# Moving ten of sixteen weight-conversion multiplies from ScalarE to GpSimd in an attention plus rational-FFN kernel

## The chip, the cores and the metric

The kernel runs on one core of a Trainium2 chip. The metric is the device time of one execution in microseconds. The core has a matrix engine (TensorE; PE in the profile, PEld its weight loads) and three engines that work on vectors: VectorE (DVE), ScalarE (ACT) and GpSimd (POOL). SyncE (SP) issues the transfers here. All engines run their own instruction queues and wait for each other by semaphores.

## The reference

Eight batches of eight heads: a packed attention of 32 queries `p` over 576 keys, then an attention of the 576 queries `q` over those 32 packed rows. The result, 4608 rows of 512, goes through a feed-forward layer with a rational activation. The two weight matrices come as float64.

```
p_packed = sm_attn(p, k, v)                 # 8 x 8 heads, 32 x 64 each
x        = sm_attn(q, p_packed, p_packed)   # 4608 x 512 after the transpose
h = x @ w_in                                # w_in  512 x 2048, float64
g = (a0 + a1 h + a2 h^2 + a3 h^3) / (1 + |b0||h| + |b1| h^2 + 1e-6)
out = g @ w_out                             # w_out 2048 x 512, float64
```

## The kernel before, in words

The feed-forward layer is walked in 128 units (batch, half of its rows, one of eight chunks of 256 hidden columns). `hidden` makes one unit: TensorE fills a PSUM tile `h`, of which there are two, ScalarE takes |h|, h² and a3·h+a2 from it, GpSimd adds `U` and `sq` (the denominator), ScalarE takes the logarithm and the exponential, and VectorE does the polynomial and the final products into `gh`, `gl` and `G`. The last VectorE products read the `h` tile and so release it for a later unit. `acc_block` multiplies a finished unit with its piece of `w_out` three units later (`LAG = 3`). The attention of a batch is split in steps that are spread between units; `m_chunk` multiplies its packed rows with `w_in`.

The weights arrive as 64-bit words. Sixteen pairs of 128-row or 256-column pieces (eight of `w_in`, eight of `w_out`; the list `words`) are loaded into borrowed buffers (`load_words`) and turned into float32 by `convert`, one pair each call: 128 partitions x 1024 words. A float64 word has a high and a low half of 32 bits, which lie side by side, so that each half is read at a step of two. The high half, read as float32, is multiplied in place by `REBIAS` = 2^-112, which moves its exponent to where float32 wants it; ScalarE scales the low half to an integer into the destination; VectorE takes the sign bits, shifts the high half left by three; and VectorE or GpSimd (GpSimd for odd pairs from the sixth on) adds the two. The first four pairs are converted after the instructions of the first attention (`PRE = 4`), one more at each unit, and more if one is due. By `words.sort` the pairs come in this order, counted from 0: `w_in` 0 to 3, `w_out` 0, 1, 2, `w_in` 4, `w_out` 3, `w_in` 5, 6, 7, `w_out` 4 to 7. Their buffers are `m` and `w`, so the profile calls the rebias of the high half `m<-m` or `w<-w` of type f32, the scaling of the low half `win<-m`, `win<-w`, `w<-w` or `half<-w` of type int32 from uint32, and the shift `m<-m` or `w<-w` of type int32.

The order of the instructions on each engine isn't the order of the program. `Planner` collects all operations, gives each a cost (`COST`, `cost`), models the time in which VectorE and GpSimd exclude each other (`shares`), simulates several list schedules (`schedule`, `order`) and emits the operations in the order of the best one. A GpSimd operation with fewer than three tensors is costed there at 135 ns plus 0.9 ns for each column. Where its plan leaves TensorE without work early in the kernel, `issue` puts in small multiplications by zero (line 290 in the profile); all planned operations are recorded at line 294.

Of the kernel before, what the change touches and what calls it, by code (L numbers as in the profile page):

```python
# [13 lines left out]
F32 = mybir.dt.float32  # L14
# [5 lines left out]
AF = mybir.ActivationFunctionType  # L20
ALU = mybir.AluOpType
# [6 lines left out]
REBIAS = 2.0**-112  # L28
# [4 lines left out]
class Planner:  # L33
# [8 lines left out]
    TRANSPOSE, F32 = (15, 0.734), (30, 1.62)  # L42
# [283 lines left out]
def attention_rational_ffn(  # L326
# [42 lines left out]
    nc = Planner(tc.nc)  # L369
# [77 lines left out]
    words_in, converted = [], 0  # L447

    def load_words(n):
        while len(words_in) < min(len(words), converted + n):  # L450
            r = len(words_in)
            kind, i, n2 = words[r]
            used = [x for x, _ in words_in]
            free = [x for x, end in room if r < end and x not in used[converted:]]
            free = [x for x in free if x[0] is not w_ring or x[1] not in (2, 3) or started]
            if not free:
                return
            x = min(free, key=lambda x: max((j for j in range(r) if used[j] == x), default=-1))
            raw = x[0].at(x[1], [P, n2 * 512], I64)
            if kind == "in":  # L460
                c = i // 2
                for y in range(2):
                    src = w_in[2 * y * P : (2 * y + 2) * P, c * CF : (c + 1) * CF].rearrange("(x p) f -> p x f", p=P)
                    nc.sync.dma_start(raw[:, 512 * y : 512 * (y + 1)].rearrange("p (x y) -> p x y", x=2), src)
            else:
                for y in range(n2):
                    nc.sync.dma_start(raw[:, 512 * y : 512 * (y + 1)], w_out[(i + y) * P : (i + y + 1) * P, :])
            words_in.append((x, raw))
# [3 lines left out]
    def undivided(c):  # L472
        if c not in X:
            pair = [i for i in UNDIVIDED if c in UNDIVIDED[i]]
            if pair:
                t = w_ring.at(pair[0], dtype=F32)
                X.update({y: t[:, x] for x, y in enumerate(UNDIVIDED[pair[0]])})
            else:
                X[c] = half_ring.at(c - 2)
        return X[c]  # L480
# [19 lines left out]
    def convert():  # L500
        nonlocal converted
        if converted == len(words):
            return
        load_words(AHEAD)
        (kind, i, n), raw = words[converted], words_in[converted][1]
        x = 4 if kind == "in" else n
        w = raw.bitcast(I32).rearrange("p (x y two) -> p x y two", x=x, two=2)
        lo, hi = w[:, :, :, 0], w[:, :, :, 1]

        if kind == "in":  # L510
            dst = win[:, i // 2]
            di = dst.bitcast(I32)
        else:
            dst = undivided(i // 2)
            di = dst.bitcast(I32)
        nc.scalar.activation(hi.bitcast(F32), hi.bitcast(F32), AF.Copy, scale=REBIAS)

        nc.scalar.activation(di, lo.bitcast(U32), AF.Copy, scale=2.0**-29)
        top = raw.bitcast(U16).rearrange("p (x y four) -> p x y four", x=x, four=4)[:, :, :, 3]
        sign = dst.bitcast(U16).rearrange("p x (y two) -> p x y two", two=2)[:, :, :, 1]  # L520
        nc.vector.tensor_scalar(sign, top, 0x8000, None, ALU.bitwise_and)
        nc.vector.tensor_scalar(hi, hi, 3, None, ALU.logical_shift_left)
        (nc.gpsimd if converted > 3 and converted % 2 else nc.vector).tensor_add(dst.bitcast(I32), hi, di)
        converted += 1
        load_words(AHEAD)
# [490 lines left out]
    for _ in range(PRE):  # L1016
        convert()
# [30 lines left out]
    for u in range(NU + LAG + 2):  # L1048
        if u < NU:
            pipe[u] = hidden(*units[u])  # L1050
        stage(u - 2)
        stage(u)
        if 0 <= u - LAG < NU:
            acc_block(u - LAG, 0)
        filler(2 * u)
        stage(u)
        stage(u - 1)
        for x in rem.get(u, ()):
            remainder(*x)
        convert()  # L1060
        while converted < len(words) and due(words[converted]) <= u + 1:
            convert()
        if 0 <= u - LAG < NU:
            acc_block(u - LAG, 1)
        if u in DIVIDE:
            divide(DIVIDE[u])
        filler(2 * u + 1)
# [78 lines left out]
```

## Time and profile before

| | |
|---|---|
| median of 3 runs | 765.33 us (764.8 to 766.16) |
| the profiled execution's own time | 765.33 us |
| its span, first to last instruction | 763.5 us |
| outside the span | 1.83 us |
| TensorE's granted clock, mean | 1.000 of full speed |

The profile is of one execution. Its busy times by engine say how full each queue was on the average; the stretches and the timelines say which was full when. On ScalarE and VectorE a recorded duration overlaps the next instruction's start, so that the step from one start to the next is the price that a full queue pays.

### The profile page before, as it was taken

How to read it: one execution, taken by the hardware profiler on the slowest of the kernel's cores; microseconds unless marked ns; L12 is line 12 of the kernel's file. 1: busy time of each engine (PE TensorE's matmuls, PEld its weight loads, DVE VectorE, ACT ScalarE, POOL GpSimd, SP SyncE). 2: the span in 40 equal slices, each digit the busy share in tenths (PEclk: the TensorE clock that was granted, in tenths of full speed). 3: DMA queues.
4: the chain of work that ended last, by engine and by line, in shares of the span. 5: the costliest groups of instructions: out<-in, count | busy, mean ns of one | idle time of the engine just before them, and what ended most of it. 6: DMA issues, size and time to landing. Idle time of an engine off the chain costs nothing.

```text
span 763.5 us, 15004 instructions
## 1 busy us (share of the span) xinstructions
PE 752.7 (99%) x5608; PEld 583.8 (76%) x5608; DVE 656.1 (86%) x1050; ACT 618.0 (81%) x1074; POOL 468.2 (61%) x457
## 2 busy tenths in 40 slices
PE   8899999999999999999999999999999999999997
PEld 7675645678788888778788887778788887778886
DVE  2889999998988889998998889998998888988773
ACT  5689986898787888988786888888786887897882
POOL 0035546986785556846695566855685655966662
PEclk9999999999999999999999999999999999999999
DMA  8994740204801137025701118122801015000001
GB/s 248 301 372 130 201 97 1 82 28 58 110 1 56 43 39 121 9 84 60 107 1 56 42 26 122 22 84 33 125 4 56 27 27 81 1 28 1 29 1 41
DMA packets 156632, 56.41 MB, mean 74 GB/s; under 512 B 126864, under 2 KB 145808, under 8 KB 156560
## 3 DMA queue, kind: packets, MB, share of 16 engines
q1 hardware_dynamic: 156560, 55.46, 33.3%
q8 instruction: 44, 0.72, 0.4%
q14 instruction: 28, 0.23, 0.1%
HBM read 46.01 MB, written 9.44 MB: 73 GB/s over the span
## 4 chain that ended last, share of the span: by engine, by line
PE 89%; DMA 4%; ACT 2%; DVE 2%; SPq 1%; POOL 1%; issue 1%; DVEq 0%; POOLq 0%; ACTq 0%
PE acc L294 46%; PE h L294 27%; PE at L294 15%; SPq L294 1%; DMA nat<-in_k_dram 1%; PE acc L290 1%; DMA w<-in_q_dram 1%; DVE Y L294 1%; DMA AH<-in_k_dram 1%; DMA w<-in_moe_w_out_dram 1%; ACT sq L294 0%; ACT U L294 0%; POOL U L294 0%; POOL gl L294 0%; ACT Y L294 0%
## 5 line engine op out<-in xcount | busy, mean ns | idle before, releaser
L294 POOL TENSOR_TENSOR U<-U,sq 128x576 f32<-128x576 f32 x128 | 185.5, 1449 | 139.2 <-ACT sq L294 135.9
L294 DVE SCALAR_TENSOR_TENSOR Y<-Y,abS,h 128x576 f32<-128x576 f32 x256 | 205.7, 804 | 55.0 <-ACT h L294 52.7
L294 PE MATMUL acc<-w,gh 128*128 128x512 f32 x736 | 240.7, 407 | 0.5 <-ACT half L294 0.5
L294 PE MATMUL h<-AH,m 128*128 128x288 f32 x1024 | 193.7, 313 | 0.7 <-DVE G L294 0.4
L294 PEld LDWEIGHTS h<-AH,m 128*128 128x128 f32 x1024 | 158.1, 188 | 28.5 <-DVE Y L294 7.1
L294 POOL TENSOR_TENSOR gl<-Y,gh 128x512 fp32r<-128x512 f32 x116 | 150.3, 1297 | 31.3 <-POOL G L294 13.6
L294 PEld LDWEIGHTS acc<-w,gh 128*128 128x128 f32 x736 | 133.6, 188 | 45.9 <-issue 16.5
L294 PE MATMUL acc<-w,gl 128*128 128x512 f32 x384 | 150.6, 411 | 0.0
L294 ACT ACTIVATE sq<-U,one 128x576 f32<-128x576 f32 x128 | 101.2, 790 | 34.9 <-POOL U L294 34.7
L294 ACT ACTIVATE U<-h 128x576 f32<-128x576 f32 x128 | 83.6, 653 | 40.3 <-PE h L294 39.9
L294 DVE TENSOR_TENSOR Y<-Y,h 128x576 f32<-128x576 f32 x128 | 95.2, 744 | 15.6 <-ACT Y L294 15.3
L294 ACT ACTIVATE h<-sq 128x576 f32<-128x576 f32 x128 | 85.1, 665 | 21.6 <-DVE Y L294 20.0
L294 PE MATMUL h<-AL,m 128*128 128x288 f32 x448 | 97.0, 296 | 0.0
L294 ACT ACTIVATE Y<-h,abS 128x576 f32<-128x576 f32 x128 | 96.7, 755 | 0.0
L294 DVE SCALAR_TENSOR_TENSOR h<-U,h 128x576 f32<-128x576 f32 x128 | 95.9, 749 | 0.0
L294 PEld LDWEIGHTS acc<-w,gl 128*128 128x128 f32 x384 | 71.8, 188 | 22.9 <-issue 10.2
L294 DVE SCALAR_TENSOR_TENSOR Y<-h,Y 128x576 f32<-128x576 f32 x116 | 86.9, 749 | 1.9
L294 ACT CAST gh<-Y 128x512 fp32r<-128x512 f32 x116 | 73.0, 629 | 14.7 <-DVE Y L294 10.1
L294 ACT ACTIVATE sq<-h 128x576 f32<-128x576 f32 x128 | 83.8, 654 | 0.0
L294 PE MATMUL acc<-half,gh 128*128 128x512 f32 x240 | 78.2, 409 | 0.2 <-ACT gh L294 0.2
L294 PEld LDWEIGHTS h<-AL,m 128*128 128x128 f32 x448 | 71.9, 188 | 2.1 <-issue 1.4
L294 PEld LDWEIGHTS acc<-half,gh 128*128 128x128 f32 x240 | 43.9, 188 | 13.5 <-issue 5.1
(149 smaller groups left out, 940.5 us busy)
## 6 DMA issues: line engine op xcount, KB each, us to landing
w<-in_moe_w_out_dram SPq DMA_DIRECT2D x16, 512.0 KB, 5.1
out_dram<-half SPq DMA_DIRECT2D x15, 512.0 KB, 2.9
nat<-in_k_dram SPq DMA_DIRECT2D x48, 144.0 KB, 4.3
nat<-in_q_dram SPq DMA_DIRECT2D x48, 144.0 KB, 4.3
nat<-in_v_dram SPq DMA_DIRECT2D x24, 256.0 KB, 3.3
m<-in_moe_w_in_dram SPq DMA_DIRECT2D x10, 512.0 KB, 9.2
w<-in_moe_w_in_dram SPq DMA_DIRECT2D x6, 512.0 KB, 8.9
nat<-in_k_dram SPq DMA_DIRECT2D x4, 512.0 KB, 7.2
```

Source lines behind the costliest of these rows:

```text
L290: getattr(self.nc.tensor, name)(*args, **kwargs)
L294: getattr(getattr(self.nc, engine), name)(*args, **kwargs)
```

## The change

For pairs 0 to 3 and for pairs 4, 6, 8, 10, 12 and 14 the multiplication of the high half by 2^-112 is issued to GpSimd as a `tensor_scalar`, on the same data in place. For the other six (5, 7, 9, 11, 13, 15) it stays on ScalarE. Nothing else in the program's text differs; the planner draws up the whole order anew with the operations on their new engine.

```
-        nc.scalar.activation(hi.bitcast(F32), hi.bitcast(F32), AF.Copy, scale=REBIAS)
+        if converted < 4 or converted % 2 == 0:
+            nc.gpsimd.tensor_scalar(hi.bitcast(F32), hi.bitcast(F32), REBIAS, None, ALU.mult)
+        else:
+            nc.scalar.activation(hi.bitcast(F32), hi.bitcast(F32), AF.Copy, scale=REBIAS)
```

## Rows read from the trace of the kernel before

**Rows 1.** The page: the span, and each engine's busy time over it.
```profile
span 763.5 us, 15004 instructions
...
PE 752.7 (99%) x5608; PEld 583.8 (76%) x5608; DVE 656.1 (86%) x1050; ACT 618.0 (81%) x1074; POOL 468.2 (61%) x457
```

**Rows 2.** Stretches: length, then busy us and instructions of PE, PEld, DVE, ACT, POOL.
```profile
29.30:41.40 12.10, 12.10 (x155) 9.27 (x140) 12.10 (x33) 7.58 (x15) 0.83 (x1) 1.00 0.89 260
41.20:82.20 41.00, 40.75 (x356) 26.69 (x354) 38.02 (x69) 40.65 (x67) 18.16 (x10) 1.00 0.71 234
82.20:100.60 18.40, 18.40 (x109) 9.73 (x109) 16.75 (x24) 18.30 (x35) 10.93 (x6) 1.00 0.89 194
...
126.00:763.00 637.00, 632.09 (x4558) 505.62 (x4558) 552.29 (x858) 518.15 (x902) 422.71 (x423) 1.00 0.27 48
```

**Rows 3.** Stretches, line 290 alone (TensorE's multiplications by zero): PE, then PEld.
```profile
41.20:82.20 41.00, 11.22 (x114) 8.90 (x112) 1.00 0.71 234
82.20:126.00 43.80, 0.05 (x1) 0.00 (x0) 1.00 0.44 103
```

**Rows 4.** Groups by form, whole span: the rebias on ScalarE, of the eleven pairs in `w`.
```profile
L294 ACT ACTIVATE w<-w 128x1024 f32<-128x1024 f32 x11 | 13.2, 1232 | 3.6 <-DMA w<-in_moe_w_out_dram 3.6
```

**Rows 5.** Groups by form, stretch 41.2 to 82.2: the rebias on ScalarE.
```profile
L294 ACT ACTIVATE w<-w 128x1024 f32<-128x1024 f32 x7 | 8.2, 1231 | 3.6 <-DMA w<-in_moe_w_out_dram 3.6
...
L294 ACT ACTIVATE m<-m 128x1024 f32<-128x1024 f32 x1 | 1.3, 1309 | 0.0
```

**Rows 6.** Timeline of ScalarE: start, duration, operation, idle before it.
```profile
33.39 1.18 ACT L294 ACTIVATE w<-w 128x1024 f32<-128x1024 f32 x1
...
34.96 1.18 ACT L294 ACTIVATE w<-w 128x1024 int32<-128x1024 uint32 x1
36.02 0.69 ACT L294 ACTIVATE kx<-kx 128x576 f32<-128x576 f32 x1
...
63.14 1.31 ACT L294 ACTIVATE m<-m 128x1024 f32<-128x1024 f32 x1
64.18 1.31 ACT L294 ACTIVATE w<-w 128x1024 f32<-128x1024 f32 x1
...
72.92 1.18 ACT L294 ACTIVATE half<-w 128x1024 int32<-128x1024 uint32 x1
...
74.10 0.71 ACT L294 ACTIVATE h<-sq 128x576 f32<-128x576 f32 x1
```

**Rows 7.** Timeline of VectorE.
```profile
34.23 0.75 DVE L294 TENSOR_TENSOR kx<-kx,small 128x576 f32<-128x576 f32 x1
...
59.62 1.25 DVE L294 TENSOR_SCALAR w<-w 128x1024 int32<-128x1024 int32 x1
...
69.98 0.71 DVE L294 TENSOR_TENSOR small<-small 128x4 f32<-128x4 f32 x1
...
74.01 1.53 DVE L294 TENSOR_SCALAR m<-m 128x1024 int32<-128x1024 int32 x1
...
75.52 0.81 DVE L294 SCALAR_TENSOR_TENSOR Y<-Y,abS,h 128x576 f32<-128x576 f32 x1
```

**Rows 8.** Tile `m` to 130 us: the shift's shortest, median and longest, in ns.
```profile
L294 DVE TENSOR_SCALAR m<-m x5: 675/701/1534, 17.9 to 74.0; 128x1024 int32<-128x1024 int32 x5
```

**Rows 9.** Groups by form, whole span: GpSimd's one-input copy and 1024-column two-input add.
```profile
L294 POOL COPY G<-Y 128x64 f32<-128x64 f32 x116 | 27.6, 238 | 36.4 <-DVE Y L294 35.6 <-ACT sq L294 0.9
...
L294 POOL TENSOR_TENSOR w<-w,w 128x1024 int32<-128x1024 int32 x3 | 7.2, 2410 | 7.0 <-DVE w L294 7.0
```

**Rows 10.** Timeline of GpSimd.
```profile
8.31 0.29 POOL L294 COPY pn<-pn 128x128 f32<-128x128 f32 x1 [6.98 <-DMA pn<-in_p_dram]
...
72.55 2.42 POOL L294 TENSOR_TENSOR win<-w,win 128x1024 int32<-128x1024 int32 x1
```

**Rows 11.** Stretches of two batches each, between the same transfers out.
```profile
263.30:436.50 173.20, 173.20 (x1320) 138.94 (x1318) 156.06 (x248) 143.34 (x254) 113.11 (x114) 1.00 0.34 57
436.50:610.30 173.80, 173.77 (x1320) 138.74 (x1318) 155.52 (x248) 143.47 (x254) 113.14 (x114) 1.00 0.32 56
```

## The prediction

> **What bounds the kernel now.** I read four views, from coarse to fine: the page, then stretches of the span, then what TensorE was given to do there, then the timelines.
>
> On the page TensorE is busy for 752.7 of 763.5 us, ScalarE for 618.0 and GpSimd for 468.2 [rows 1]. Taken alone this says that ScalarE doesn't matter. It is an average over stages, and the conversions all lie in one early stage: eleven rebias instructions work on `w` and the other five on `m` [rows 4], and eight of the sixteen start between 41.2 and 82.2 us [rows 5].
>
> By stretches there are three stages [rows 2]. From 29.3 to 41.4 VectorE is busy for all of 12.1 us, and ScalarE for 7.58. From 41.2 to 82.2 ScalarE is busy for 40.65 of 41.0 us and VectorE for 38.02. From 126 us on TensorE is busy for 632.09 of 637.0 us.
>
> TensorE looks busy in the middle stage as well, 40.75 of 41.0 us. The reader must see what it is busy with: 11.22 us of that are multiplications by zero, which the program puts where its plan has nothing for TensorE [rows 3]. From 82.2 to 126 there are 0.05 us of them. So up to 82.2 us TensorE waits for ScalarE and VectorE, and behind that it catches up on work that it already has. A microsecond gained ahead of 82.2 is kept, since TensorE has nothing idle in which it could be lost again; one gained on ScalarE behind 82.2 is hidden by TensorE's own queue.
>
> **The change part by part.** The profiled execution took 765.33 us, 1.83 more than its span, and is equal to the median of the runs; the sum is made against 765.33.
>
> *What ScalarE loses.* Where its queue is full, one rebias costs the step to the next start: 64.18 - 63.14 = 1.04 us [rows 6]. Ten go, 10.4 us. I count them by stage, with the order of the pairs.
> - Pairs 0 to 3 stand in the opening, up to about 30 us, where ScalarE has room. I take 0 for them.
> - Pair 4 is the one at 33.39. Behind it an exponential of the first attention starts at 36.02, though the subtraction that feeds it ended at 34.23 + 0.75 = 34.98 [rows 6, 7]. ScalarE was late by up to 1.04 us there. But VectorE, which has the next step, is full over this whole stretch. I take 0, and keep 1.04 as the other bound.
> - Eight rebias instructions lie in 41.2 to 82.2 [rows 5]: pairs 5 to 12. Pairs 6, 8, 10 and 12 move. ScalarE is relieved by 4 x 1.04 = 4.2 us where it is full.
> - Pair 14 comes behind 82.2. TensorE's queue covers it: 0, and 1.04 if that cover were gone.
>
> *What VectorE allows.* With 4.2 us less on ScalarE the next to be late is VectorE. In the stage it has 41.0 - 38.02 = 2.98 us of idle time [rows 2], and its work there doesn't shrink. So the stage can shorten by 2.98 us at most, before what follows.
>
> *What GpSimd adds.* The trace has no multiplication by a constant on GpSimd. Below it is bounded by the one-input copy: 0.238 us for 64 columns and 0.29 for 128 [rows 9, 10], so 0.052 us for 64 more, and for 1024 columns 0.238 + 15 x 0.052 = 1.02 us. Above it is bounded by the two-input add of 1024 columns on the same strided words, 2.41 us [rows 9]. One input is what it has in common with the copy, so I take 1.02; the program's plan reckons with 0.135 + 1024 x 0.0009 = 1.06. GpSimd has 41.0 - 18.16 = 22.84 us free in the stage [rows 2], and 4 x 1.02 = 4.1 fit.
>
> [...]
>
> *What GpSimd does to VectorE.* The shift at 74.01 takes 1.53 us; the median of its kind is 0.701 [rows 7, 8]. Just in front of it GpSimd began an add at 72.55 that ended at 74.97 [rows 10]; the shift ends at 75.54, that is 0.57 later. It stood still until GpSimd was done, and lost 0.83 us. Two more in the stage are long in this way: a shift of 1.25 us, 0.55 too long, and an operation on four columns of 0.71 us [rows 7], where I put the excess at 0.55 as well. That is 1.9 us over ten GpSimd instructions [rows 2], 0.2 us each. Four more cost VectorE 0.8 us; the bounds are 0, and 0.83 each, 3.3 us.
>
> [...]
>
> *The new waits.* The shift, and behind it all later VectorE work of the queue, now waits for GpSimd in place of ScalarE. On GpSimd the `U` addition of a unit can stand behind a rebias, and ScalarE's logarithm waits for it. In return the rebias no longer stands ahead of the low half on the same engine, so a pair can be ready about 1.04 us earlier. I count these as even. No transfer is added or moved in the program; a buffer comes free when its pair is added up, as before.
>
> *The sum.* The stage shortens by the smaller of ScalarE's relief, 4.2 us, and VectorE's room, 2.98 - 0.8 = 2.2 us. The forecast is 765.33 - 2.2 = 763.1 us.
>
> **How much the new order blurs it.** Every cost that changes makes the planner draw up the whole order anew. Two stretches of two batches each, with the same 1320 TensorE instructions, take 173.2 and 173.8 us [rows 11]: the same work in two orders differs by 0.6. Over the 637 us from 126 on, 3.7 times as long, that is 2.2 us if all differences add and 1.2 if they are independent (0.6 times the root of 3.7). So I blur each case by 1.2 us. A measurement of this kernel can tell about 0.2% from no change, 1.5 us.
>
> **The rivals.**
>
> *Hidden anyway.* ScalarE is full because the planner fills gaps with conversions, not because the units are held up by them. For it: two rebias instructions stand back to back at 63.14 and 64.18 [rows 6], which reads like filling. Against it: at 72.92 a low-half scaling of 1.18 us stands directly ahead of the exponential at 74.10 on which VectorE's product at 75.52 waits [rows 6, 7], so conversions do hold up units. [...]
>
> *Full relief.* VectorE's idle time isn't the limit, because the new order also takes blocked time out of it and uses the start: 4 x 1.04 in the middle stage and 1.04 by the exponential at 36.02, 5.2 us, to 760.1. For it: 11.22 us of TensorE time are free to be won [rows 3]. Against it: VectorE's full opening.
>
> *Slower: GpSimd's price.* The instruction takes 2.41 us, like the two-input add, and the plan thinks 1.06. Each of the four in the middle stage then delivers 1.35 us late, with a `U` addition behind it on GpSimd and a shift on VectorE waiting; ScalarE's and VectorE's queues stand in their planned order meanwhile. That is 4 x 1.35 = 5.4 us against the gain of 2.2: 765.33 + 3.2 = 768.5. It decides from the duration at which 4 x (d - 1.06) = 2.2, d = 1.61 us. For it: every GpSimd row of 1024 columns is at 2.41. Against it: the one-input copies.
>
> *Slower: the order.* GpSimd's multiplication is as cheap as a copy, but the new order of the long stage from 126 on is 2.2 us worse, and nothing is won in front: 767.5 [rows 11].
>
> **How the numbers follow.** The forecast at 763.1 has a chance of 0.50, hidden anyway 0.20, full relief 0.12, slower by GpSimd's price 0.12, slower by the order 0.06. Blurred by 1.2 us to either side, the forecast alone spans 761.9 to 764.3; a fifth of that, 0.11 of its 0.50, lies above 763.8, where it counts as no change. So faster by over 0.2%: 0.39 + 0.12 = 0.51; within it: 0.11 + 0.20 = 0.31; slower: 0.12 + 0.06 = 0.18. The range that leaves out no more than 2 in 10 goes from 759.8, just past full relief, to 767.4, short of the case of GpSimd's price and about at that of the order.
>
> **What would show each step.** ScalarE should have six f32 rebias instructions left and GpSimd ten new ones, near 1.0 us each; a mean over 1.6 makes the slower rival. ScalarE's busy time between the first `h` and about 80 us should fall by some 4 us for the same units, and VectorE's idle time there close to zero: if VectorE keeps its 2.98 us, VectorE wasn't the limit. TensorE's multiplications by zero should fall from 11.22 us by about the gain. The unit at which they cease should begin some 2 us earlier, and the end should move by as much; a difference that appears only behind 126 us is the order's and not the change's. [...] I am wrong if GpSimd's price is over 1.6 us, if the units' rhythm before 82 us stays although ScalarE has gaps, or if the long stage comes out different by more than 2 us.

## The result, and the profile after

The changed kernel takes 769.62 us (median of six runs, 768.73 to 771.11) against 765.75 us before in the same comparison: a ratio of 1.0055, 95% interval 1.0042 to 1.0069. It is slower by 3.9 us where 2.2 us less was forecast, and outside the range of 759.8 to 767.4. The profiled execution is the longest of the six, 771.11 us, 1.5 above the median, so differences between the two profiles are larger than those of the medians.

The page of the changed kernel, against [rows 1]:

```profile
span 769.3 us, 14938 instructions
...
PE 750.2 (98%) x5568; PEld 581.1 (76%) x5568; DVE 663.0 (86%) x1050; ACT 609.9 (79%) x1064; POOL 496.4 (65%) x467
```

ScalarE lost ten instructions and 8.1 us. GpSimd gained ten and 28.2 us, almost 3 us each. VectorE has the same 1050 instructions and is busy for 6.9 us longer: the timelines below show it standing still inside instructions.

The same stretches of the changed kernel as in [rows 2]:

```profile
29.30:41.40 12.10, 11.27 (x156) 7.89 (x141) 11.47 (x29) 5.67 (x12) 6.25 (x3) 1.00 0.87 219
41.20:82.20 41.00, 37.59 (x257) 24.50 (x256) 39.18 (x60) 35.38 (x59) 28.51 (x14) 1.00 0.73 240
...
126.00:763.00 637.00, 634.03 (x4547) 505.42 (x4547) 558.65 (x872) 522.09 (x909) 424.20 (x424) 1.00 0.26 47
```

In the middle stage ScalarE was relieved as intended, from 40.65 to 35.38 us of 41.0. Nothing came of it: VectorE has 60 instructions there in place of 69 and was busy for longer. A relieved ScalarE beside a slower stage means that ScalarE's queue doesn't limit the changed kernel there; whether it did before is asked below, by leaving its work out.

GpSimd's groups by form up to 135 us:

```profile
L294 POOL TENSOR_SCALAR w<-w 128x1024 f32<-128x1024 f32 x6 | 18.6, 3105 | 1.7 <-DMA w<-in_moe_w_in_dram 0.9 <-DMA w<-in_moe_w_out_dram 0.8
L294 POOL TENSOR_SCALAR m<-m 128x1024 f32<-128x1024 f32 x4 | 11.9, 2978 | 13.1 <-DMA m<-in_moe_w_in_dram 13.1
```

The new instruction takes 3.0 to 3.1 us. The forecast took 1.02 and had 2.41 as its upper bound [rows 9].

VectorE's timeline in the changed kernel, and below it GpSimd's at the same places:

```profile
62.83 1.34 DVE L294 TENSOR_SCALAR w<-w 128x1024 int32<-128x1024 int32 x1
...
67.40 2.38 DVE L294 TENSOR_SCALAR half<-w 128x1024 uint16<-128x1024 uint16 x1
...
78.63 1.26 DVE L294 TENSOR_TENSOR small<-small 128x4 f32<-128x4 f32 x1
```

```profile
60.54 3.08 POOL L294 TENSOR_SCALAR w<-w 128x1024 f32<-128x1024 f32 x1 [0.92 <-DMA w<-in_moe_w_in_dram]
...
66.75 2.41 POOL L294 TENSOR_TENSOR win<-w,win 128x1024 int32<-128x1024 int32 x1
...
77.42 2.45 POOL L294 TENSOR_TENSOR half<-w,half 128x512 fp32r<-128x512 f32 x1 [0.63 <-DVE G L294]
```

Add start and duration on both sides: the shift ends at 64.17, GpSimd's rebias at 63.62; the sign instruction at 69.78, GpSimd's addition at 69.16; the four columns at 79.89, GpSimd's addition at 79.87. Each VectorE instruction waited out a GpSimd one that had begun before it. The first is held by a moved rebias itself, the other two by additions that the program had before too and that now stand at other places.

TensorE's multiplications by zero fell from 33.34 us (332 instructions) to 28.93 (292) in the whole kernel, while the kernel became slower. The prediction had named their fall as a sign of the gain. They are put in where the plan sees a hole, so they tell what the plan thinks, not what was won, and once put in they run.

### The profile page after: what moved, and what is told of

It reads as the page before. It is cut to its first block, busy times and chain, and to the rows that moved or that the text cites. A ratio compares the mean times of both kernels' runs of the same rounds, so it can differ in the third digit from the quotient of the medians.

```text
span 769.3 us, 14938 instructions
## 1 busy us (share of the span) xinstructions
PE 750.2 (98%) x5568; PEld 581.1 (76%) x5568; DVE 663.0 (86%) x1050; ACT 609.9 (79%) x1064; POOL 496.4 (65%) x467
## 4 chain that ended last, share of the span: by engine, by line
PE 83%; DVE 6%; ACT 3%; issue 2%; DMA 2%; SPq 2%; POOL 1%; ACTq 0%; DVEq 0%; POOLq 0%
PE acc L294 44%; PE h L294 25%; PE at L294 14%; DVE Y L294 2%; SPq L294 2%; DVE small L294 2%; DMA m<-in_moe_w_in_dram 1%; DMA AH<-in_k_dram 1%; ACT sq L294 1%; DVE half L294 1%; ACT Y L294 1%; ACT U L294 1%; ACT kx L294 1%; DVE h L294 1%; DVE win L294 0%
```

## The experiments

Each ratio is against the kernel before, run on the same chip beside it. In the diffs, "moved" marks operations that are planned as one thing and issued as another, by a few lines in `issue`:

```
             waiting.discard(i)
+            if i in self.moved:
+                x = calls[0][1][0]
+                self.nc.gpsimd.tensor_scalar(x, x, REBIAS, None, ALU.mult)   # or as said below
+                continue
```

and in `convert`, behind the rebias, which is recorded for ScalarE as before:

```
+        if converted < 4 or converted % 2 == 0:
+            nc.moved.add(len(nc.ops) - 1)
```

The order is then the one of the kernel before, instruction by instruction on each engine, and only the engine of the ten differs.

### What the multiplication costs by itself

A kernel of single instructions, two of each kind (loops cut, notes added):

```
nc.gpsimd.tensor_scalar(high(t[0]), high(t[0]), 0.5, None, ALU.mult)           # ta: step of two
for m in (256, 512, 1024):
    nc.gpsimd.tensor_scalar(t[1][:, 0:m], t[1][:, 0:m], 0.5, None, ALU.mult)   # tb: dense
nc.gpsimd.tensor_copy(t[2][:, 0:1024], t[2][:, 1024:2048])                     # tc: dense
nc.gpsimd.tensor_copy(high(t[3]), ones)                                        # td: step of two
nc.gpsimd.tensor_tensor(high(t[4]), high(t[4]), ones, ALU.mult)                # te: step of two
nc.gpsimd.tensor_scalar(high(t[7]), high(t[7]), REBIAS, None, ALU.mult)        # th
```

> Leaves out the whole computation: only single instructions on 128 partitions, one after the other, to get their prices. Theory A (the price is that of the operation, a multiplication by a constant on GpSimd): dense 1024 columns cost near 3.0 us as the strided ones do, and a strided copy costs near 1.0. Theory B (the price is that of the step of two): dense 1024 columns cost near 1.0 us, and the strided copy is near 3.0 as well. A strided two-input multiplication should be near the 2.41 us of the add.

Groups by form of this kernel:

```profile
L40 POOL TENSOR_SCALAR ta<-ta 128x1024 f32<-128x1024 f32 x2 | 5.7, 2856 | 6.9 <-DMA ta<-in_q_dram 6.9
L55 POOL TENSOR_SCALAR th<-th 128x1024 f32<-128x1024 f32 x2 | 5.7, 2856 | 0.1
L43 POOL TENSOR_SCALAR tb<-tb 128x1024 f32<-128x1024 f32 x2 | 5.5, 2771 | 0.2
L49 POOL TENSOR_TENSOR te<-te,ones 128x1024 f32<-128x1024 f32 x2 | 4.8, 2386 | 0.1
L47 POOL COPY td<-ones 128x1024 f32<-128x1024 f32 x2 | 3.0, 1498 | 0.1
L43 POOL TENSOR_SCALAR tb<-tb 128x512 f32<-128x512 f32 x2 | 3.0, 1491 | 0.2
...
L45 POOL COPY tc<-tc 128x1024 f32<-128x1024 f32 x2 | 2.1, 1040 | 0.1
L43 POOL TENSOR_SCALAR tb<-tb 128x256 f32<-128x256 f32 x2 | 1.7, 850 | 20.8 <-DMA tb<-in_q_dram 20.7
```

From 256 to 1024 dense columns the multiplication grows by 1921 ns, 2.5 ns for each column; the step of two adds 85 ns, and the factor adds nothing. So the price is in the main the operation's own. The dense copy of 1024 columns costs 1.04 us, close to the 1.02 that the prediction worked out from small copies [rows 9, 10]. Written at a step of two, as the rebias is, a copy costs 1.50 us, so even for a copy 1.02 was too little. And a multiplication by a constant isn't priced like a copy at all: at the step of two it costs 2.86 us, more than a multiplication of two tensors, 2.39 us.

### What the plan knows

If the loss came from a plan that thinks 1.06 us, a plan with the measured price should mend it. Three kernels, for all ten pairs, for pairs 0 to 3 alone, and for the other six alone:

```
-            fixed, per = 135, 0.9
+            fixed, per = (150, 2.78) if name == "tensor_scalar" else (135, 0.9)
...
-        if converted < 4 or converted % 2 == 0:
+        if converted < 4:                                 # first four
+        if converted >= 4 and converted % 2 == 0:         # later six
```

> The changed kernel, with the plan told that the new GpSimd instruction takes 3.0 us in place of 1.06. Theory A (the loss comes from a plan that is wrong by 1.9 us for each of ten instructions): the loss goes, 765.7 or below, down to 763.5. Theory B (the loss comes from the 30 us of GpSimd time themselves, which hold VectorE's shared operations and the opening): 768 to 770, much like the changed kernel.

> Only pairs 0 to 3 on GpSimd, with the plan told 3.0 us. In the trace of the changed kernel the first hidden unit is 3 us late. If the opening makes that loss by itself, 768 to 769 here and the first h near 40 us; if the loss is made by the six later pairs, 765 to 766.

> Only pairs 4, 6, 8, 10, 12 and 14 on GpSimd, with the plan told 3.0 us. If the later pairs gain what the prediction said, once the plan knows the price, 763 to 764.5. If GpSimd's hold on VectorE eats the relief of ScalarE, 765.5 to 768.

All ten: 781.59 us, 1.0215 [1.0201, 1.0229]. The first four: 768.81, 1.0047 [1.0033, 1.0061]. The later six: 777.12, 1.0160 [1.0147, 1.0174]. The theory fell: with the right price the planner makes a far worse kernel. In the kernel with the first four the first two transfers out start at 143.32 and 167.61 us, as before (143.35 and 168.04), and only the third is late, 207.90 against 203.99. That is long behind the conversions, and so the order's doing. Why the planner draws so badly with a true price was not settled; these three can't tell the engine's effect from the order's. The next runs hold one of them fixed.

### Order and engine taken apart

One kernel with the old order and the ten multiplications issued to GpSimd (the diff above), and one with the order of the changed kernel and the ten issued to ScalarE, where `issue` calls

```
+                self.nc.scalar.activation(x, x, AF.Copy, scale=REBIAS)
```

> All engines keep the order of the kernel before (drawn up with the ten rebias operations on ScalarE); only the ten instructions themselves are issued to GpSimd, at their place in that order. Theory B (GpSimd's 30 us hurt by themselves): 768 to 773. Theory C (the change costs mostly by the new order of everything else): 764 to 766.5.

> The other half of that pair: all engines keep the order of the changed kernel (drawn up as if GpSimd did the rebias in 1.06 us), but the ten instructions are issued to ScalarE as before. Theory B: 765 to 767, most of the loss is gone. Theory C: 768 to 770, the loss stays.

| | ten on ScalarE | ten on GpSimd |
|---|---|---|
| order of before | 765.25 | 768.42, 1.0047 [1.0034, 1.0060] |
| order of after | 767.30, 1.0032 [1.0020, 1.0044] | 769.62, 1.0055 [1.0042, 1.0069] (against 765.75) |

By the medians each alone loses: the engine 3.2 us, the order 2.1, which lies between the two ranges expected for it. Together 3.9, somewhat less than the sum. Starts of the same transfers out, in us, show where:

| transfer | before | GpSimd, old order | ScalarE, new order | after |
|---|---|---|---|---|
| first | 143.35 | 146.58 | 144.78 | 147.76 |
| second | 168.04 | 171.27 | 169.59 | 172.57 |
| third | 203.99 | 207.23 | 208.24 | 211.19 |
| last whole batch | 610.28 | 613.32 | 613.44 | 616.33 |

These are single executions; the two with the new order ran 1.2 and 1.5 us above their medians, so the order's share reads larger in the last row (3.2 us) than by the medians (2.1). Go along the rows. From the first column to the second it is 3.23, 3.23, 3.24 and 3.04; from the third to the fourth 2.98, 2.98, 2.95 and 2.89. The engine costs 3 us in either order, all of it ahead of the first transfer, and hardly any is lost or given back later. The order costs 1.4 us ahead of the first transfer, 2.7 more between the second and the third, and about 1.1 comes back by the last. Stretches between these transfers, of the kernel with the new order on ScalarE and then of the changed kernel:

```profile
0.00:144.78 144.78, 134.37 (x1112) 83.33 (x1112) 117.02 (x212) 114.47 (x195) 59.93 (x50) 1.00 0.61 178
...
169.59:208.24 38.65, 38.63 (x313) 31.47 (x320) 34.54 (x55) 31.63 (x57) 26.76 (x28) 1.00 0.57 83
```

```profile
0.00:147.76 147.76, 134.68 (x1112) 83.89 (x1112) 124.24 (x212) 105.11 (x185) 91.48 (x60) 1.00 0.60 174
...
172.57:211.19 38.62, 38.62 (x313) 31.48 (x320) 34.54 (x55) 31.59 (x57) 26.75 (x28) 1.00 0.52 83
```

Ahead of the first transfer both do the same 212 VectorE instructions; beside GpSimd's ten they take 7.2 us longer. In the stretch shown behind it the two agree to 0.1 us. The new order's stretch of 38.6 us has TensorE full, as has the old one's of 35.95 us; so that stretch is long by what TensorE is given there and not by a wait, as far as the profile tells.

Is 2.1 us for an order large? Two kernels on ScalarE with the plan's price of the rebias changed by 5 ns, which only draws the order anew:

```
+            fixed += 5 * (kwargs.get("scale") == REBIAS)     # the other: -5
```

> The kernel before, with the plan's price of the rebias on ScalarE raised by 5 ns and nothing else: the same instructions on the same engines, in another drawn-up order. It prices the drawing itself. The prediction took 1.2 us to either side for this. If the order's share in the loss is of that kind, the time moves by 1 to 5 us to some side; if orders hardly matter, 764.5 to 766.

> The kernel before, with the plan's price of the rebias on ScalarE lowered by 5 ns and nothing else: a second sample of how much the drawing of an order moves the time by itself. Raised by 5 ns it gave 0.9989 (0.9978 to 1.0001). I expect 763 to 767; beyond that, the 2.1 us of the changed kernel's order would be no more than scatter.

764.30 us, 0.9989 [0.9978, 1.0001], and 764.70, 0.9996 [0.9987, 1.0006]. Two redrawn orders stay within 1 us, the first a little below the range expected if orders hardly matter. So 2.1 us isn't the ordinary scatter of these two draws, though two draws are few.

### What relief is worth

If ScalarE's full queue is the limit, taking the ten instructions away must bring what the prediction summed up. First with the old order, so that nothing else moves. The correction of the exponent goes into VectorE's sign instruction, whose median is 0.75 us in both kernels:

```
+            if i in self.moved:
+                continue
...
+        if converted < 4 or converted % 2 == 0:
+            nc.vector.tensor_scalar(sign, top, 0x8000, 0x4000, ALU.bitwise_and, ALU.bitwise_or)
```

Then the same with the order drawn anew, for ten and for all sixteen.

> The order of the kernel before, with the ten rebias instructions left out; the bit they set is put in by VectorE's sign instruction, which has a second operation free (and 2^30 is then part of the sum of the halves; numbers below 2^-126 would come out wrong). It prices ScalarE's relief alone. If ScalarE's queue sets the middle stage, as the prediction said, 761 to 763.5; if the conversions only fill its gaps, 764.5 to 766.

> The same ten rebias instructions left out in the same way, with a new order drawn up for it. If the relief is worth something and the planner can use it, at or below the kernel with the frozen order, 759 to 763; if a new order costs by itself, above it, 765 to 769.

> All sixteen rebias instructions left out of ScalarE (as with ten: VectorE's sign instruction sets the bit), with a new order. ScalarE loses 16.6 us of work in the first 113 us. If its queue were the limit anywhere there, 758 to 762; if its conversions only fill gaps, 763.5 to 766, the order's scatter aside.

Ten left out, old order: 765.08, 0.9993 [0.9983, 1.0003]. Ten, new order: 764.33, 0.9992 [0.9983, 1.0001]. Sixteen: 765.58, 1.0001 [0.9991, 1.0011]. No gain clear of the noise, three times; by the intervals 1.3 us at the most, where 2.2 were forecast. (The second lies between the two ranges expected for it.) In the first of them, the middle stage and ScalarE's waits from 41.2 to 100.6 us:

```profile
41.20:82.20 41.00, 40.40 (x350) 26.47 (x350) 37.71 (x67) 38.15 (x65) 17.33 (x10) 1.00 0.69 226
```

```profile
ACT w L297 <- DMA w<-in_moe_w_out_dram: 4.0, 1, 4.0
ACT U L297 <- PE h L297: 1.1, 2, 0.6
ACT kx L297 <- DVE small L297: 1.0, 1, 1.0
ACT h L297 <- DVE Y L297: 0.8, 1, 0.8
ACT ppT L297 <- PE at L297: 0.5, 1, 0.5
```

Before, ScalarE waited for that transfer (3.6 us, a wait that ends as the stage begins) and 0.3 us for `h`, and for nothing else. Now it waits for TensorE, VectorE and again TensorE in turn: the relief turned into waits for the others, piece by piece. The `h` tiles start 0.3 us earlier than before at 64.32 and 78.55 (64.61 and 78.83), 0.4 at 117.76 (118.19), and no more.

Was VectorE the limit in its place? The sign instruction of the ten pairs is left out, old order:

```
+        if converted < 4 or converted % 2 == 0:
+            nc.moved.add(len(nc.ops) - 1)        # behind the sign instruction; issue skips it
```

> The kernel before in its own order, rebias on ScalarE, but with VectorE's sign instruction of the same ten pairs left out (weights lose their signs): VectorE has about 10 x 0.65 = 6.5 us less to do, ScalarE as much as ever. If VectorE is what the early stage really waits for, as the long VectorE instructions suggest, 760 to 763.5. If the turn of the two h tiles sets the rhythm and neither engine's queue does, 764 to 765.5.

765.43, 0.9994 [0.9985, 1.0003]. VectorE's waits from 41.2 to 100.6 us:

```profile
DVE Y L297 <- ACT Y L297: 5.4, 5, 1.8
DVE Y L297 <- ACT h L297: 1.9, 3, 1.4
```

They were 2.6 and 1.1 before. The two engines hand each other work by turns, and either one's relief becomes a wait for the other.

What the two wait for in the end, the trace of the kernel before shows. First TensorE's waits from 41.2 to 126 us, then pieces of the chain of work that ended last (start, duration, what):

```profile
PE h L294 <- DVE G L294: 0.4, 1, 0.4
PE at L294 <- ACT m L294: 0.3, 1, 0.3
```

```profile
47.76 0.66 PE at L294 x4
...
75.76 2.43 PE acc L290 x28
...
78.45 0.45 PE acc L290 x4
78.90 2.14 PE h L294 x8
...
120.38 0.02 issue
```

From 47.76 to 120.38 us the chain lies on TensorE alone, and the multiplications by zero (line 290) are part of it. They were put into TensorE's queue when the order was drawn up and run in their turn, whether or not there is a hole by then: 332 before, 332 with the ten rebias instructions left out. With them TensorE waits for other engines for 0.7 us in all in 84.8 us. In the middle stage, TensorE's multiplications by zero with ten rebias instructions left out, and the whole stage with ten sign instructions left out:

```profile
41.20:82.20 41.00, 10.79 (x108) 8.63 (x108) 1.00 0.69 226
```

```profile
41.20:82.20 41.00, 41.00 (x360) 27.15 (x359) 36.28 (x66) 40.26 (x66) 17.72 (x10) 1.00 0.71 229
```

By this reading TensorE's queue, filled up by multiplications by zero, sets the pace of the old order there, and a shorter queue on ScalarE or VectorE has nothing to win. It is read from the traces and not tested: a kernel without these multiplications was not run, and what the relief would be worth then stays open.

Then I relieved both: no rebias and no sign for any pair, order drawn anew.

```
-        nc.scalar.activation(hi.bitcast(F32), hi.bitcast(F32), AF.Copy, scale=REBIAS)
-        nc.vector.tensor_scalar(sign, top, 0x8000, None, ALU.bitwise_and)
```

> Both instructions are left out for all sixteen pairs, the rebias on ScalarE and the sign on VectorE (and the shift goes right in place of left, which keeps the numbers finite; the weights are wrong), with a new order. ScalarE has 16.6 us less to do in the early stage and VectorE about 10.4. If the two queues limit the stage together, each filling the other's gaps, 755 to 761. If the turn of the two h tiles or TensorE's own work limits it, 762.5 to 765.5.

764.27, 0.9981 [0.9971, 0.9990]: 1.0 us between the medians and 1.4 by the ratio, for some 27 us of work taken off the two. (ScalarE loses 16 steps of 1.04 us, VectorE 16 of about 0.65, as from 82.03 to 82.67 in the kernel before.) The middle stage, and TensorE's multiplications by zero in it:

```profile
41.20:82.20 41.00, 39.27 (x349) 26.02 (x348) 36.20 (x58) 33.32 (x58) 21.90 (x12) 1.00 0.78 266
```

```profile
41.20:82.20 41.00, 10.91 (x114) 9.18 (x114) 1.00 0.78 266
```

Neither engine is full any longer, and 10.91 us of multiplications by zero are still there, as good as the 11.22 of before [rows 3]: the planner put in as many anew. Shorter queues on ScalarE and VectorE don't win them back. In this order the chain of work that ended last lies on TensorE only from 69.87 us on; before that it has landings of weight transfers in turn with VectorE and ScalarE, one of them 7.8 us. Whether the transfers limit that part was not tried.

### Is it the price, or the moved dependence?

The ten rebias instructions are left out as above, old order, and in their places GpSimd multiplies by one a part of a buffer that isn't in use at that time and for which nobody waits, with 1024 columns or 336 (the part is set to zero once, at the start):

```
+            if i in self.moved:
+                x = self.scratch[:, :, 64 : 64 + 64]      # the other: 64 + 21
+                self.nc.gpsimd.tensor_scalar(x, x, 1.0, None, ALU.mult)
+                continue
```

> The kernel with the old order and the ten rebias instructions left out, and at the ten places in GpSimd's queue a multiplication by one on 1024 columns of a tile that nobody reads in that time. Nobody waits for its result, so that only GpSimd's queue and its hold on VectorE are left of the change (the first five start as soon as GpSimd is free, earlier than the rebias did). Theory L (the hold on VectorE and the queue make the loss): 767 to 769, with long VectorE instructions beside the ten. Theory D (the loss is the conversion itself, which waits 3 us for its high half): 764.5 to 766.

> The same with 336 columns in place of 1024, about 1.05 us each by the prices measured (0.85 us for 256 columns, 1.49 for 512), which is the price that the prediction took. Theory L: a third or less of the loss, 765 to 766.2. If it loses as much as the long one, the number of instructions counts and not their length.

Long: 766.40, 1.0023 [1.0014, 1.0032], 1.3 us between the medians and 1.8 by the ratio. Short: 764.83, 1.0000 [0.9990, 1.0011]. The later instructions on GpSimd's timeline, long and then short:

```profile
60.09 3.21 POOL L296 TENSOR_SCALAR G<-G 128x1024 f32<-128x1024 f32 x1
74.97 2.77 POOL L296 TENSOR_SCALAR G<-G 128x1024 f32<-128x1024 f32 x1
80.09 2.79 POOL L296 TENSOR_SCALAR G<-G 128x1024 f32<-128x1024 f32 x1
```

```profile
59.67 1.51 POOL L296 TENSOR_SCALAR G<-G 128x336 f32<-128x336 f32 x1
74.61 1.34 POOL L296 TENSOR_SCALAR G<-G 128x336 f32<-128x336 f32 x1
78.31 1.08 POOL L296 TENSOR_SCALAR G<-G 128x336 f32<-128x336 f32 x1
```

The ten take 1.14 us on the mean when short, near the price that the prediction took, and then GpSimd's queue and its hold on VectorE cost nothing that the runs can show. The long ones take 2.96 us on the mean and cost 1.3 to 1.8, though no conversion waits for them: the queue and the held VectorE are enough for that. The 766.40 lies between the ranges expected from the two theories, which fits a loss made by both. Against the kernel of the same order with the ten left out, `h` starts 0.1 later at 64.40, 0.8 later at 79.32 and 1.8 later at 94.71, and the distance stays. The rest up to 3.2 us I put down to the waits of the conversions themselves; that is the difference of two runs, not shown by one.

### Which pairs

Old order, GpSimd for pairs 0 to 3 alone (`if converted < 4`) or for the other six alone:

> The order of the kernel before; only pairs 0 to 3 issued to GpSimd. In the trace with all ten issued so, the first h is 1.1 us late and stays so until 67 us. If the opening makes that third of the loss by itself: 766 to 766.7, all milestones about 1 us late. If it was pair 4 that made it: 765 to 765.5.

> The order of the kernel before; only pairs 4, 6, 8, 10, 12, 14 issued to GpSimd. If GpSimd's hold on VectorE between 67 and 95 us makes two thirds of the loss: 766.5 to 767.8, the first h near 37, and the loss there between the h of 67 and the one of 95 us.

The first four: 765.14, 0.9996 [0.9988, 1.0005]; I had expected a loss, and there is none. The later six: 768.12, 1.0031 [1.0020, 1.0042], 0.3 us above the range expected. So most of the engine's loss is theirs, 2.5 us of 3.2 by the medians; the first transfer out starts 2.69 us late (146.04) in place of 3.23. The rest would be the first four's, beside the six; but the intervals of the two runs overlap. One place, in VectorE's and then GpSimd's timeline of the kernel with the later six:

```profile
83.22 1.15 DVE L299 TENSOR_SCALAR w<-w 128x1024 int32<-128x1024 int32 x1
84.29 1.98 DVE L299 TENSOR_SCALAR win<-w 128x1024 uint16<-128x1024 uint16 x1
86.16 1.20 DVE L299 CUSTOM_DVE_ANT_0 half<-w,half 128x2048 uint16<-128x2048 uint16 x1
```

```profile
80.86 2.96 POOL L296 TENSOR_SCALAR w<-w 128x1024 f32<-128x1024 f32 x1
83.92 1.72 POOL L299 TENSOR_TENSOR U<-U,sq 128x576 f32<-128x576 f32 x1
```

and the same instructions of VectorE and GpSimd in the kernel before:

```profile
81.43 0.70 DVE L294 TENSOR_SCALAR w<-w 128x1024 int32<-128x1024 int32 x1
82.03 0.76 DVE L294 TENSOR_SCALAR win<-w 128x1024 uint16<-128x1024 uint16 x1
82.67 1.21 DVE L294 CUSTOM_DVE_ANT_0 half<-w,half 128x2048 uint16<-128x2048 uint16 x1
```

```profile
83.77 1.41 POOL L294 TENSOR_TENSOR U<-U,sq 128x576 f32<-128x576 f32 x1 [5.72 <-ACT sq L294]
```

Before, GpSimd had been idle for 5.72 us when the `U` addition came, and VectorE's two instructions ran through. Now the rebias ends at 83.82; the shift waits it out and ends at 84.37. GpSimd starts the `U` addition at 83.92, before the shift has ended. So the sign instruction behind the shift waits as well: the addition ends at 85.64, the sign instruction at 86.27. The two instructions went from 1.24 us to 2.94 (start of the first to start of the next): one GpSimd instruction lost VectorE 1.7 us, the larger part by the addition that stood behind it. Up to the first transfer out VectorE is busy for 125.30 us in place of 119.68, 5.6 us more for six instructions, with 216 of its own in both. `h` starts 1.2 us late at 80.01 and 2.3 late at 95.63, where TensorE waits for VectorE. And the chain of work that ended last, which lay on TensorE alone there before, lies on VectorE from 83.09 to 120.74 us (with all ten moved, from 83.90 to 96.39).

## Why the prediction was wrong

**What bounds the kernel: failed, and with it the gain.** "A microsecond gained ahead of 82.2 is kept" was right as far as it goes: losses there are kept whole, to the end. But "up to 82.2 us TensorE waits for ScalarE and VectorE" was read from busy queues and from multiplications by zero taken for free time. They are instructions in TensorE's queue, and with them TensorE waited for others for 0.7 us in all from 41.2 to 126; the "11.22 us of TensorE time" that the rival of full relief called "free to be won" were not free. ScalarE's relief by itself is worth nothing that the runs can show (three runs), VectorE's by itself nothing (one run), and both together 1.0 to 1.4 us. So even at the price that the forecast took, no gain is in sight: the short multiplications, for which no conversion waits, give 1.0000.

**The sum, "the smaller of ScalarE's relief, 4.2 us, and VectorE's room", 2.2 us: the failed term.** It treats a full engine's busy time as a length that can be cut off. With the ten left out and nothing else moved, the time is 0.9993 of before [0.9983, 1.0003], not to be told from no change. "Hidden anyway", the case of no change, with a chance of 0.20, was right in this: ScalarE's conversions filled time in which it would have waited for VectorE and TensorE.

**What GpSimd adds: mis-sized, and with it the loss.** 1.02 us was taken from the copy; 2.86 us was measured alone and 3.0 to 3.1 in the kernel, beyond the upper bound of 2.41. The small copies from which 1.02 was worked out are dense, and at a step of two a copy takes 1.50. The likeness in the number of inputs decided for the copy, and it misled; the same engine's only rows of 1024 columns had been nearer.

**What GpSimd does to VectorE: seen rightly, mis-sized.** 0.2 us for each instruction was taken, 0.83 was the upper bound; the later six cost VectorE 5.6 / 6 = 0.9 us each. That VectorE stands still until GpSimd is done is seen again at 62.83 us: the shift takes 1.34 us where the median before was 0.70 [rows 8], 0.64 us lost. What the prediction didn't see is the second wait, for the work queued behind the long instruction: at 83 us VectorE lost 1.7 us in all to the two.

**The new waits, "I count these as even":** not even, as far as the difference between 3.2 us with the conversions waiting and 1.3 to 1.8 with nobody waiting tells; no run shows them by themselves.

**The opening at 0 and pair 14 at 0:** the opening right, shown by the first four alone; beside the later six they may add some 0.5 us (3.23 against 2.69 at the first transfer out, in one execution of each). Pair 14 alone wasn't tried.

**The rival "Slower: GpSimd's price"** named the mechanism, and its 768.5 us is what the old order gives (768.42), but by two errors that cancel: its delays, by the measured 3.0 us, would be 4 x (3.0 - 1.06) = 7.8 us, and the gain set against them was 2.2. Measured are 3.2 and 0. That the number came near is luck. Its turning point of 1.61 us fits with no loss at 1.14 us and 1.3 to 1.8 us lost at 2.96, without being located by them.

**The order, blurred by 1.2 us:** enough for a plan whose prices barely change (two draws within 1 us), too little for one in which operations change the engine: 2.1 us with the plan's price, and up to 16.6 us over the kernel before with the true one, where engine and order act together.

## What to carry to other kernels

That an engine's queue is full doesn't say that relieving it gains anything: leave the work out, in the old order, and measure that before moving it anywhere. Work that a program puts into a queue to fill holes is work of that queue: look whether the engine waits, not whether what it does is useful. Price an operation on its new engine by the operation itself, not by one with as many inputs (here 2.86 us, where 1.02 was worked out from copies), and count against GpSimd not only its own duration but what is queued behind it: here VectorE lost 1.7 us to both in a row. Where a planner redraws the order, compare engine and order separately, two by two, and read the loss between the same transfers out.

## What was not expected of the hardware

A multiplication by a constant on GpSimd costs 2.77 us for 1024 dense columns, 2.7 times a copy (1.04) and more than a product of two tensors on strided words (2.39). And VectorE lost to GpSimd twice running: at 83 us it waited out a rebias that ended at 83.82 and then, with 0.1 us between GpSimd's two instructions, the next one, until 85.64, as well.
